# Chunked linear attention with a highway layer on one core: query rows of 2 KB, joint 64-row turns, compact state, gate in SBUF, a new order

## The chip, the core and the metric

The kernel runs on one core of a Trainium2 chip. Its engines have queues of their own and run beside each other: TensorE (PE; its weight loads are listed as PEld), VectorE (DVE), ScalarE (ACT), GpSimd (POOL) and SyncE (SP), which here issues DMAs. The metric is the device time of one execution in microseconds, as the median of several runs.

## What is computed

Four batches, eight heads, 768 positions, head size 64. Attention goes in blocks of 64 positions with a decay `lam` per head and a state that is carried from block to block; a highway layer follows on the 3072 x 512 result.

```python
for b in range(nb):                       # blocks of 64 positions
    qb, kb, vb = q[:, :, sl], k[:, :, sl], v[:, :, sl]
    intra = einsum('bhic,bhjc->bhij', qb, kb) * Dmask[None]      # lam**(i-j) for i >= j
    intra = einsum('bhij,bhjd->bhid', intra, vb)
    inter = einsum('bhid,bhde->bhie', qb * lam_pow[None], kv_state)
    out[:, :, sl] = intra + inter
    kv_state = lam_block * kv_state + einsum('bhsd,bhse->bhde', kb * rev_pow, vb)
# x: (B*S, H*D)
H = maximum(x @ w_h, 0);  T = sigmoid(x @ w_t + b_t)
result = T * H + (1 - T) * x
```

Inputs and the result are float32. The kernel may choose its own blocks: a mask with the decay and a carried state give the same result at any block length.

## The kernel before

The kernel splits each batch into three tiles of 256 positions, twelve tiles n in all, and each tile into two blocks b of 128. Within a tile, partition p holds positions 2p and 2p+1 (index j), so that one 512 B row of q, k or v (two positions of one head) goes to one partition, and block b is one half of the partitions. Instead of a decay matrix it scales queries by lam to the power t and values by lam to the power -t, t counted in the batch, in the cast from float32 to bf16 (`cast_q`, `cast_v`; `cast_k` only casts). The scores then need only a 0/1 mask `tri`, and the state is a plain sum that stays in one PSUM bank `kv` for a whole batch. Heads go in pairs hp, e being the head in the pair.

Steps of one tile:
- `load` of q, k and v, each in two halves of four heads (256 KB), all on SP's queue; `load_w` of the two weight matrices in halves of 512 KB.
- `trans` turns k and q with an identity on the full 128x128 array, eight per tile and operand; `evac_k` and `evac_q` copy them from PSUM, the second reordering positions.
- `score` and `state` run as 64x64 pieces of the array, interleaved in `scores_state`; `mask` multiplies scores by `tri` on DVE.
- `evac_s` copies the state (128x512, a head pair's own 64x64 blocks on the diagonal and zeros beside them), `inter` multiplies it with the queries, eight full-array matmuls per tile (none for the first block of a batch), and `intra` adds the masked scores times the values into the same bank `o`.
- `take` copies `o` to bf16 `xT`. The highway layer works on `xT` in four blocks per tile of eight matmuls each (`block`: h and t for each half u), then `relu` (DVE: max(h,0) - x), `sigm` (ACT, in place in PSUM), `gate` (DVE: times the sigmoid), and `turns` adds x and the gated part while turning back to rows; `evac_r` and `store_r` put out 512 KB per tile. The last tile goes in two halves, with `turn`, `evac_o` and `store`.

The order of every engine's work is written out by hand in the string PLAN. A token names a step, its arguments, the engine after @ and the PSUM banks after =: Lk, Lq, Lv loads; W, WC weights and their casts; CK, CQ, CV casts; TK, TQ turns; EK, EQ their evacuation; SS, S, U scores and state; KE state copy; M mask; I inter; A intra; D take; F block; H relu; G sigmoid; X gate; R turn back; E evacuation; ST store; Z filler matmuls on an all-zero tile. Each engine takes its instructions in the order of the string and waits, in order, for what each needs. Work tiles come from pools whose buffer counts are in BUFS, seven PSUM banks are numbered 0 to 6, and the eighth is `kv`.

Of the kernel before, what the change touches and what calls it, by code (L numbers as in the profile page):

```python
# [22 lines left out]
WC.0.1.0@POOL D.0.1@ACT Lv.2.1 WC.0.1.1@DVE Z.4=0 SS.1.0=01 M.1.1.1 I.1=35 KE.1.1@ACT Lv.2.0 F.0.0.0=4 WC.1.1.0@DVE PT
M.1.0.1 Lk.3.1 F.0.1.0=6 M.1.0.0 WC.1.0.0@POOL WC.1.0.1@ACT Lk.3.0 WC.1.1.1@DVE A.1.1 A.1.0 BC F.0.0.1=1 H.0.1 Lq.3.1
D.1.1@ACT H.0.0 D.1.0@ACT F.0.1.1=0 Lq.3.0 CQ.2.2@POOL F.1.0.0=2 Lv.3.0 G.0.1@ACT CK.2.2@DVE F.1.0.1=6 Lv.3.1
G.0.0@ACT X.0.1@DVE TQ.2.2=5 Lq.4.0 X.0.0@DVE TK.2.2=4 EQ.2.2@ACT CV.2.2@POOL F.1.1.0=3 Lq.4.1 EK.2.2@DVE G.1.0@ACT
H.1.0 SS.2.0=01 Lk.4.1 H.1.1 CK.3.2@POOL SS.2.1=54 Lk.4.0 M.2.0.1 F.1.1.1=2 KE.2.0@ACT M.2.1.0 Lv.4.0 TK.3.2=3 M.2.1.1
CQ.3.2@POOL G.1.1@ACT I.2=15 M.2.0.0 Lv.4.1 A.2.1 X.1.0@DVE A.2.0 Lk.5.0 R.0=40 D.2.0@ACT D.2.1@DVE CV.3.2@POOL
TQ.3.2=6 E.0.0@ACT Lk.5.1 F.2.1.1=1 E.0.1@ACT EQ.3.2@DVE Lq.5.1 EK.3.2@ACT X.1.1@DVE F.2.1.0=5 CQ.4.2@POOL Lq.5.0
R.1=40 H.2.1 SS.3.1=62 Lv.5.0 F.2.0.0=3 CK.4.2@POOL KE.3.0@ACT M.3.1.1 Lv.5.1 E.1.1@ACT M.3.1.0 SS.3.0=52 E.1.0@ACT  # L30
H.2.0 Lq.6.0 TQ.4.2=0 KE.3.1@ACT CV.4.2@POOL M.3.0.1 TK.4.2=6 G.2.1@ACT Lq.6.1 F.2.0.1=4 M.3.0.0 EQ.4.2@ACT EK.4.2@DVE
Lv.6.0 I.3=32 A.3.0 CK.5.2@POOL A.3.1 Lk.6.1 SS.4.1=56 D.3.0@ACT D.3.1@DVE TK.5.2=0 KE.4.0@ACT M.4.1.1 Lk.6.0
F.3.0.0=2 G.2.0@ACT CQ.5.2@POOL EK.5.2@DVE Lv.6.1 SS.4.0=36 H.3.0 F.3.0.1=0 Lq.8.0 M.4.0.0 CV.5.2@POOL M.4.0.1
TQ.5.2=2 Lk.9.0 G.3.0@ACT F.3.1.0=3 X.2.1@DVE Lq.7.0 EQ.5.2@ACT X.2.0@DVE F.3.1.1=6 CQ.6.2@POOL M.4.1.0 Lq.7.1
KE.4.1@ACT I.4=14 H.3.1 G.3.1@ACT R.2=25 Lk.8.1 X.3.0@DVE A.4.0 E.2.1@ACT X.3.1@DVE A.4.1 Lk.7.1 SS.5.0=30 E.2.0@ACT
D.4.0@DVE CK.6.2@POOL SS.5.1=56 D.4.1@ACT Lk.7.0 TQ.6.2=2 M.5.0.0 KE.5.0@ACT CV.6.2@POOL TK.6.2=1 M.5.1.1 Lv.7.0
EQ.6.2@ACT F.4.1.0=4 M.5.0.1 Lv.7.1 EK.6.2@ACT F.4.0.0=3 H.4.1 Lk.8.0 M.5.1.0 I.5=62 SS.6.1=01 H.4.0 Lq.8.1 A.5.0
KE.6.0@ACT M.6.1.0 CQ.7.2@POOL R.3=45 Lv.9.1 A.5.1 M.6.1.1 SS.6.0=30 D.5.0@ACT Lv.8.0 F.4.0.1=1 M.6.0.0 D.5.1@ACT
M.6.0.1 Lk.9.1 TQ.7.2=6 G.4.0@ACT CK.7.2@POOL F.5.0.0=3 Lq.10.1 EQ.7.2@ACT F.4.1.1=2 H.5.0 Lk.10.1 E.3.1@ACT X.4.0@DVE
TK.7.2=0 CV.7.2@POOL G.4.1@ACT I.6=63 ST.0 KE.6.1@DVE F.5.0.1=5 X.4.1@DVE Lv.8.1 F.5.1.0=1 G.5.0@ACT CK.8.2@POOL  # L40
EK.7.2@DVE Lq.9.0 A.6.0 E.3.0@ACT H.5.1 A.6.1 SS.7.1=20 Lq.9.1 D.6.0@ACT D.6.1@DVE TK.8.2=4 M.7.1.1 F.6.1.0=1 Lv.9.0
EK.8.2@ACT X.5.0@DVE CK.9.2@POOL F.6.1.1=6 KE.7.0@DVE Lk.10.0 CQ.8.2@POOL H.6.1 R.4=30 SS.7.0=54 Lk.11.1 E.4.0@ACT
F.5.1.1=1 E.4.1@ACT M.7.0.1 G.6.1@ACT ST.4 M.7.1.0 TK.9.2=3 Lq.10.0 M.7.0.0 TQ.8.2=0 G.5.1@ACT CV.8.2@POOL F.6.0.0=4
EQ.8.2@DVE Lk.11.0 KE.7.1@ACT X.5.1@DVE I.7=25 EK.9.2@ACT Lq.11.0 A.7.0 H.6.0 A.7.1 CQ.9.2@POOL SS.8.0=01 X.6.1@DVE
D.7.1@ACT Lv.10.1 SS.8.1=34 M.8.0.1 D.7.0@ACT F.6.0.1=6 KE.8.0@DVE Lq.11.1 CK.10.2@POOL F.7.0.0=5 M.8.1.0 G.6.0@ACT
M.8.1.1 ST.3 TQ.9.2=1 CV.9.2@POOL H.7.0 F.7.1.0=2 EQ.9.2@ACT Lv.10.0 X.6.0@DVE TK.10.2=3 M.8.0.0 ST.1 I.8=45
EK.10.2@ACT CQ.10.2@POOL H.7.1 SS.9.1=61 A.8.1 KE.9.0@ACT M.9.1.0 A.8.0 R.5=02 M.9.1.1 SS.9.0=36 CK.11.2@POOL
E.5.1@DVE F.7.0.1=1 KE.9.1@ACT M.9.0.1 E.5.0@ACT F.7.1.1=2 D.8.0@DVE D.8.1@ACT ST.5 CQ.11.2@POOL M.9.0.0 G.7.0@ACT
Lv.11.1 TK.11.2=6 Lv.11.0 I.9=04 F.8.1.0=5 EK.11.2@ACT ST.2 X.7.0@DVE TQ.10.2=3 G.7.1@ACT H.8.1 CV.10.2@POOL F.8.0.0=1
EQ.10.2@ACT R.6=65 H.8.0 A.9.1 X.7.1@DVE A.9.0 SS.10.1=31 D.9.0@ACT D.9.1@DVE F.8.1.1=2 E.6.1@ACT M.10.1.1 F.9.1.0=0  # L50
E.6.0@DVE G.8.1@ACT M.10.1.0 ST.6 TQ.11.2=4 CV.11.2@POOL KE.10.0@DVE F.9.1.1=5 EQ.11.2@ACT X.8.1@DVE SS.10.0=16
G.9.1@ACT H.9.1 R.7=32 M.10.0.1 KE.10.1@ACT F.8.0.1=4 X.9.1@DVE E.7.0@ACT M.10.0.0 E.7.1@ACT I.10=06 SS.11.0=53
# [365 lines left out]
```

## Time and profile before

| | |
|---|---|
| median of three runs | 110.14 us (109.15 to 110.21) |
| profiled execution | 107.8 us span |
| instructions | 4970 |
| read from HBM / written | 20.98 MB / 6.29 MB |
| score masks on DVE, 48 | 31.0 us, 680 ns each |
| scales of q and v on POOL, 23 | 42.6 us, some 1.9 us per 1024 columns |
| sigmoids on ACT, 52 | 22.0 us |
| matmuls of the highway layer, 416 | 49.5 us |
| filler matmuls, 45 | 12.4 us |

The span is the time from the first to the last instruction of one profiled execution. Busy time of an engine is the union of its instructions; matmuls overlap each other, so the length of one record is not its share of PE's time: the distance between starts is. A line such as L299 is a line of the kernel. An arrow `out<-in` names the tiles. A group's idle time is the time that its engine stood still just before its instructions.

### The profile page before, as it was taken

How to read it: one execution, taken by the hardware profiler on the slowest of the kernel's cores; microseconds unless marked ns; L12 is line 12 of the kernel's file. 1: busy time of each engine (PE TensorE's matmuls, PEld its weight loads, DVE VectorE, ACT ScalarE, POOL GpSimd, SP SyncE). 2: the span in 40 equal slices, each digit the busy share in tenths (PEclk: the TensorE clock that was granted, in tenths of full speed). 3: DMA queues.
4: the chain of work that ended last, by engine and by line, in shares of the span. 5: the costliest groups of instructions: out<-in, count | busy, mean ns of one | idle time of the engine just before them, and what ended most of it. 6: DMA issues, size and time to landing. Idle time of an engine off the chain costs nothing.

```text
span 107.8 us, 4970 instructions
## 1 busy us (share of the span) xinstructions
PE 99.5 (92%) x2190; PEld 80.7 (75%) x2190; DVE 83.5 (77%) x140; ACT 70.1 (65%) x129; POOL 55.6 (52%) x46
## 2 busy tenths in 40 slices
PE   4986999999999999999999999999999999999950
PEld 1332665588987888889879888979898788899940
DVE  1133495879798987999975997999977998958860
ACT  3303254685875588499568766957697798587940
POOL 6028340427977988689529583999593600000000
PEclk9999999999999999999999999999999999999998
DMA  0899999999999999999999999999999444108264
GB/s 3 221 302 289 291 357 384 327 286 284 290 298 264 298 280 303 284 293 263 288 277 272 297 333 285 294 272 303 361 325 290 152 182 161 40 6 317 78 240 149
DMA packets 42701, 27.59 MB, mean 256 GB/s; under 512 B 1588, under 2 KB 38712, under 8 KB 42680
## 3 DMA queue, kind: packets, MB, share of 16 engines
q1 hardware_dynamic: 42528, 27.27, 86.7%
q8 instruction: 17, 0.28, 1.0%
q14 instruction: 4, 0.03, 0.1%
q10 hardware_dynamic: 152, 0.01, 0.1%
HBM read 20.98 MB, written 6.29 MB: 253 GB/s over the span
## 4 chain that ended last, share of the span: by engine, by line
PE 74%; DVE 10%; DMA 5%; issue 3%; POOL 1%; SPq 1%; ACT 1%; POOLq 0%; DVEq 0%
PE bt L299 18%; PE bh L299 17%; PE bs L216 7%; PE bx L346 6%; PE bo L281 6%; DMA qf<-in_q_dram 5%; DVE m L255 5%; PE bqtr L203 5%; PE bspin L365 5%; PE bktr L203 4%; PE bo L271 3%; DVE hm L304 2%; DVE th L317 2%; PE kv L221 2%; POOL qb L189 1%
## 5 line engine op out<-in xcount | busy, mean ns | idle before, releaser
L299 PEld LDWEIGHTS <-w_b 128*128 128x128 bf16 x416 | 36.4, 98 | 5.0 <-issue 0.5
L255 DVE TENSOR_TENSOR m<-bs,tri 128x512 bf16<-128x512 f32 x48 | 31.0, 680 | 2.9 <-PE bs L216 2.3
L189 POOL TENSOR_TENSOR qb<-qf,pow_q 128x1024 bf16<-128x1024 f32 (+1 forms) x13 | 23.6, 1812 | 9.5 <-DMA qf<-in_q_dram 8.7
L313 ACT ACTIVATE bt<-bt,bt_col 128x256 f32<-128x256 f32 (+1 forms) x52 | 22.0, 432 | 7.5 <-PE bt L299 4.1
L299 PE MATMUL bh<-xT,w_b 128*128 128x256 bf16 (+1 forms) x208 | 25.0, 265 | 0.0
L299 PE MATMUL bt<-xT,w_b 128*128 128x256 bf16 (+1 forms) x208 | 24.5, 265 | 0.4 <-DVE th L317 0.2
L189 POOL TENSOR_TENSOR vs<-vf,pow_v 128x1024 bf16<-128x1024 f32 x10 | 19.0, 1902 | 7.4 <-DMA vf<-in_v_dram 6.5
L304 DVE SCALAR_TENSOR_TENSOR hm<-bh,xT 128x512 bf16<-128x512 f32 (+1 forms) x26 | 16.5, 643 | 3.3 <-PE bh L299 2.4
L317 DVE TENSOR_TENSOR th<-bt,hm 128x512 bf16<-128x512 f32 (+1 forms) x26 | 16.4, 642 | 2.0 <-ACT bt L313 1.9
L216 PE MATMUL bs<-qT,kT 64*64 64x128 bf16 x384 | 14.0, 218 | 0.4
L365 PE MATMUL bspin<-blank,id 128*128 128x512 bf16 x45 | 12.4, 420 | 1.4 <-POOL id masks.py:199 1.4
L103 POOL CAST kb<-kf 128x1024 bf16<-128x1024 f32 (+1 forms) x10 | 9.9, 994 | 7.1 <-DMA kf<-in_k_dram 7.1
L101 ACT ACTIVATE ss<-kv 128x512 bf16<-128x512 f32 x15 | 9.0, 597 | 6.3 <-PE bs L216 5.1
L216 PEld LDWEIGHTS <-kT 64*64 64x64 bf16 x384 | 10.9, 106 | 2.6 <-issue 1.1
L101 ACT ACTIVATE xT<-bo 128x512 bf16<-128x512 f32 x16 | 9.2, 597 | 4.8 <-PE bo L281 4.8
L101 ACT ACTIVATE o<-bx 128x512 f32<-128x512 f32 x19 | 10.5, 596 | 1.3 <-PE bx L346 1.3
L101 ACT ACTIVATE qT<-bqtr 128x1024 bf16<-128x1024 bf16 (+1 forms) x10 | 9.8, 980 | 1.8 <-PE bqtr L203 1.8
L281 PE MATMUL bo<-m,vs 64*64 64x128 bf16 x384 | 9.3, 219 | 0.7 <-DVE m L255 0.4
L365 PEld LDWEIGHTS <-id 128*128 128x128 bf16 x45 | 4.4, 106 | 6.6 <-issue 1.9
L221 PE MATMUL kv<-vs,kb 64*64 64x64 bf16 x320 | 9.3, 196 | 0.0
L203 PE MATMUL bqtr<-id,qb 128*128 128x128 bf16 x96 | 7.5, 220 | 0.9 <-POOL qb L189 0.9
L281 PEld LDWEIGHTS <-vs 64*64 64x64 bf16 x384 | 6.5, 106 | 2.4 <-issue 1.6
(50 smaller groups left out, 110.1 us busy)
## 6 DMA issues: line engine op xcount, KB each, us to landing
kf<-in_k_dram SPq DMA_DIRECT2D x24, 256.0 KB, 5.5
vf<-in_v_dram SPq DMA_DIRECT2D x24, 256.0 KB, 5.4
qf<-in_q_dram SPq DMA_DIRECT2D x24, 256.0 KB, 5.5
out_dram<-o SPq DMA_DIRECT2D x11, 512.0 KB, 3.8
w_f<-in_moe_w_h_dram SPq DMA_DIRECT2D x2, 512.0 KB, 6.6
w_f<-in_moe_w_t_dram SPq DMA_DIRECT2D x2, 512.0 KB, 8.6
out_dram<-oh SPq DMA_DIRECT2D x2, 128.0 KB, 2.0
out_dram<-oq SPq DMA_DIRECT2D x1, 256.0 KB
```

Source lines behind the costliest of these rows:

```text
L101: A.activation(dst, src, AF.Copy)
L189: ENG[eng].tensor_tensor(dst, in0=get(src, n)[:, heads(p)].rearrange("p h (j d) -> p h j d", j=J), in1=pw[:, n % NST, heads(p), :, None].t ...
L203: T.transpose(t[:, i, j, :], get(x + "b", n)[:, j, h:h + 2, :], id128)
L216: T.matmul(get("s", n, e, hp // 2)[half(b), hp % 2, j, :], lhsT=get("kT", n)[half(e), hp, j, half(b)], rhs=get("qT", n)[half(e), hp, b * C ...
L221: T.matmul(kv[half(e), hp, half(e)], lhsT=get("kb", n)[half(b), j, 2 * hp + e, :], rhs=get("vs", n)[half(b), 2 * hp + e, j, :], start=firs ...
L255: V.tensor_tensor(new(("m", n, e, u), [128, 2, J, C]), in0=get("s", n, e, u), in1=tri[:, None].to_broadcast([128, 2, J, C]), op=ALU.mult)
L281: T.matmul(get("o", n, b)[half(e), hp, :], lhsT=get("vs", n)[half(b), 2 * hp + e, j, :], rhs=get("m", n, e, u)[half(b), hp % 2, j, :], sta ...
L299: T.matmul(t[:, r, :], lhsT=w_b[w][:, kc, (2 * u + r) * 128:(2 * u + r + 1) * 128], rhs=get("xT", *g)[:, kc, :], start=(kc == 0), stop=(kc ...
L304: V.scalar_tensor_tensor(new(("hm", g, u), [128, 2, z * C], tag=f"hm{z}"), in0=get("h", g, u), scalar=0.0, in1=get("xT", *g)[:, 2 * u:2 * ...
L313: A.activation(dst[:, r, :], src[:, r, :], AF.Sigmoid, bias=bt_col[:, 2 * u + r:2 * u + r + 1])
L317: ENG[eng].tensor_tensor(new(("th", g), [128, NP, z * C], tag=f"th{z}")[:, 2 * u:2 * u + 2, :], in0=get("tt", g, u), in1=get("hm", g, u), ...
L365: T.matmul(t, lhsT=id128, rhs=blank, start=True, stop=True)
```

## The change

- Queries: partition p now holds eight positions of both heads of a pair, so that the row of a head is 2 KB. One load of 512 KB brings a whole tile (`load_q`). In a half of the partitions, p is made of 16 groups of eight positions and four head pairs.
- Turns: `trans_k` and `trans_q` work on halves of 64 partitions, 16 instructions each per tile, and write into two banks that k and q share, one per block b; `evac_kq` copies each bank (128x1024) in one go. Query positions lie in the order (t, group) afterwards; `tri` is built in that order and `take` puts it right.
- State: `kv` is 128x256, without the zero blocks; `inter` goes as 64x64 pieces, 16 per tile.
- Gate: the sigmoid writes a bf16 tile in SBUF, and 17 of 26 gates are on POOL, nine on DVE.
- lam comes as one row; a matmul with ones spreads it over the partitions (`spread`), and `powers` makes the two tables of powers, the query one per partition by a selection.
- Tiles that rotate are allocated once and taken in turn (`new`).
- PLAN is another order, with other engines for some steps and 25 fillers instead of 45; BUFS has other counts.

Counts by engine in the orders: EK and EQ 17 ACT and 9 DVE (four of the first tile's in halves) become EB 14 ACT and 10 DVE; D 16 ACT and 8 DVE become 21 and 3; E 20 ACT and 5 DVE become 14 and 11; whole-tile or half-tile CK 2 ACT, 1 DVE, 10 POOL become 6 ACT and 8 POOL.

```diff
 PLAN = """
-Lk.0.0 Lv.0.1 Lv.0.0 Lq.0.0 Lk.0.1 Lq.0.1 Lv.1.1 CK.0.0@POOL Lq.1.0 Z.12=0 TK.0.0=0 Lq.1.1 CV.0.0@DVE Lk.1.0
-CQ.0.0@POOL EK.0.0@DVE Lv.1.0 CV.0.1@DVE CK.0.1@ACT Lk.1.1 Z.11=1 TQ.0.0=1 B=2 EQ.0.0@ACT CQ.0.1@POOL W.0.1 W.0.0
...
-F.12.1.1=5 G.10.0@ACT X.10.1@DVE F.11.1.1=1 F.11.1.0=0 G.12.1@ACT X.10.0@DVE F.11.0.1=2 G.11.1@ACT H.11.1 F.12.1.0=4
-R.10=36 G.11.0@ACT H.12.1 X.11.1@DVE F.11.0.0=0 E.10.0@ACT X.12.1@DVE F.12.0.1=4 E.10.1@ACT H.11.0 F.12.0.0=1
-G.12.0@ACT X.11.0@DVE ST.10 R.11.1.1=5 H.12.0 R.11.0.2=3 E.11.1.1@DVE X.12.0@DVE E.11.0.2@ACT ST.11.1.1 R.11.1.0=0
-ST.11.0.2 E.11.1.0@DVE ST.11.1.0
+LM=0 PW Lv.0.0 Lv.1.0 Lk.0.0 Lq.0 CV.0.0@POOL CQ.0.1@DVE Lk.0.1 CQ.0.0@POOL CK.0.0@ACT Z.18=1 TQ.0=12 Lv.0.1 PT
+CV.0.1@DVE CK.0.1@POOL Lq.1 Lk.1.0 Lk.1.1 TK.0=12 EB.0.0@DVE Lv.1.1 EB.0.1@ACT Z.4=3 SS.0.1=34 W.0.1 CQ.1.1@DVE
+KE.0.0@ACT CQ.1.0@DVE CK.1.1@ACT M.0.1.1 Z.1=5 SS.0.0=56 CV.1.0@POOL M.0.1.0 M.0.0.1 I.0=01 TQ.1=24 CK.1.0@POOL TK.1=24
+B=3 CV.1.1@POOL KE.0.1@ACT WC.0.1.0@POOL EB.1.1@DVE EB.1.0@ACT Z.2=6 SS.1.1=64 M.0.0.0 W.0.0 Lq.2 A.0.0 Lk.2.0 A.0.1
+WC.0.1.1@POOL KE.1.0@DVE M.1.1.0 Lk.2.1 I.1=25 Lv.2.0 WC.0.0.0@POOL M.1.1.1 D.0.1@ACT WC.0.0.1@POOL D.0.0@ACT Lv.2.1
+SS.1.0=61 M.1.0.1 W.1.0 KE.1.1@ACT CQ.2.2@POOL F.0.0.0=0 M.1.0.0 H.0.0 W.1.1 A.1.1 WC.1.0.1@POOL F.0.1.0=4 Lq.3
...
+F.11.1.1=0 E.7.1@DVE ST.5 E.9.1@ACT E.8.1@ACT G.10.0 F.12.0.1=2 X.10.0@POOL F.12.0.0=1 F.11.1.0=3 G.11.1 E.8.0@DVE
+X.10.1@DVE H.12.0 F.11.0.0=5 ST.7 F.11.0.1=4 R.10=01 E.9.0@DVE H.11.0 F.12.1.0=6 H.11.1 G.12.0 X.11.1@POOL ST.8
+F.12.1.1=2 G.11.0 X.11.0@POOL X.12.0@DVE E.10.0@ACT E.10.1@DVE R.11.1.0=5 G.12.1 ST.9 E.11.1.0@ACT ST.10 ST.11.1.0
+H.12.1 R.11.0.2=3 E.11.0.2@ACT ST.11.0.2 X.12.1@DVE R.11.1.1=4 E.11.1.1@DVE ST.11.1.1
 """
-BUFS = dict(kf=5, qf=5, vf=5, kb=3, qb=2, vs=3, kT=2, qT=2, m=8, xT4=2, th4=2, xT2=3, xT1=2, th2=2, th1=2, hm2=3, hm1=2, tb2=2, tb1=2, ss=4, o=5, oh=2, oq=1)
+BUFS = dict(kf=5, qf=5, vf=5, kb=3, qb=3, vs=4, kq=3, m=8, xT2=4, xT1=2, th2=3, th1=2, hm2=4, hm1=4, tb2=4, tb1=4, ss=6, o=5, oh=2, oq=1)
...
-    kv = ps.tile([128, NP, 128], F32, tag="kv", name="kv", bufs=1)
-    V.memset(kv, 0.0)
+    kv = ps.tile([128, NP, D], F32, tag="kv", name="kv", bufs=1)
...
-            made[key] = sb.tile(shape, dtype, tag=tag, name=tag, bufs=BUFS[tag])
+            i = turn_of.get(tag, 0)
+            turn_of[tag] = (i + 1) % BUFS[tag]
+            if (tag, i) not in kept:
+                kept[tag, i] = singles.tile(shape, dtype, name=f"{tag}{i}")
+            made[key] = kept[tag, i]
...
+    def load_q(n):
+        b, c = divmod(n, NST)
+        nc.sync.dma_start(out=new(("qf", n), [128, 2, QT * D], F32),
+                          in_=q[b, :, c * 2 * C:(c + 1) * 2 * C, :].rearrange("h (g t) d -> g h (t d)", t=QT))
...
+    def trans_k(n, bk):
+        turn_banks(n, bk)
+        for hp in range(NP):
+            for j in range(J):
+                for b in range(2):
+                    i = (hp * J + j) * 64
+                    T.transpose(get("tr", n, b)[:, i:i + 64], get("kb", n)[half(b), j, 2 * hp:2 * hp + 2, :], id128[half(b), half(b)])
+
+    def trans_q(n, bk):
+        turn_banks(n, bk)
+        for t in range(QT):
+            for b in range(2):
+                T.transpose(get("tr", n, b)[:, KN:].rearrange("p (hp t g) -> p hp t g", hp=NP, t=QT)[:, :, t, :],
+                            get("qb", n)[half(b), t], id128[half(b), half(b)].rearrange("p (g hp) -> p hp g", hp=NP))
+
+    def evac_kq(n, b, eng):
+        copy(eng, new(("kq", n), [128, 2, 1024])[:, b], get("tr", n, b))
...
-        for b in range(2):
-            if n % NST or b:
-                for hp in range(NP):
-                    T.matmul(get("o", n, b)[:, hp, :], lhsT=get("ss", n, b)[:, hp, :],
-                             rhs=get("qT", n)[:, hp, b * C:(b + 1) * C],
-                             start=hp == 0, stop=False, skip_group_check=True)
-                begun.update((n, b, e) for e in range(2))
+        for hp in range(NP):
+            for x in range(2):
+                for e in range(2):
+                    b = e ^ x
+                    if n % NST or b:
+                        T.matmul(get("o", n, b)[half(e), hp, :], lhsT=get("ss", n, b)[half(e), hp, :], rhs=qT(n, b, hp)[half(e)],
+                                 start=o_first(n, b, e), stop=False, skip_group_check=True)
...
-        copy(eng, new(("xT", *g), [128, NP, z * C], tag=f"xT{z}")[:, :, r * C:(r + 1) * C], get("o", n, b))
+        copy(eng, new(("xT", *g), [128, NP, z * C], tag=f"xT{z}")[:, :, r * C:(r + 1) * C].rearrange("p h (g t) -> p h g t", t=QT),
+             get("o", n, b).rearrange("p h (t g) -> p h g t", t=QT))
...
+            A.activation(new(("tb", g, u), [128, 2, z * C], BF16, tag=f"tb{z}")[:, r, :], get("t", g, u)[:, r, :], AF.Sigmoid,
+                         bias=bt_col[:, 2 * u + r:2 * u + r + 1])
...
+    def spread(bk):
+        T.matmul(bank(("lm",), bk[0], [128, H]), lhsT=ones, rhs=lam_r, start=True, stop=True)
+
+    def powers():
+        A.activation(ln_bc, get("lm"), AF.Ln)
+        V.tensor_tensor(p_lnv, in0=ln_bc[:, None, :, None].to_broadcast([128, NST, H, J]),
+                        in1=tk_f[:, :, None, :].to_broadcast([128, NST, H, J]), op=ALU.mult)
+        A.activation(pow_v, p_lnv, AF.Exp, scale=-1.0)
+        V.tensor_tensor(ln_sel, in0=ln_bc.rearrange("p (hp e) -> p e hp", e=2), in1=sel[:, None, :].to_broadcast([128, 2, NP]), op=ALU.mult)
+        V.tensor_reduce(ln_q, ln_sel, axis=mybir.AxisListType.X, op=ALU.add)
+        V.tensor_tensor(p_lnq, in0=ln_q[:, None, :, None].to_broadcast([128, NST, 2, QT]),
+                        in1=tq_f[:, :, None, :].to_broadcast([128, NST, 2, QT]), op=ALU.mult)
+        A.activation(pow_q, p_lnq, AF.Exp)
```

More of the change, by code (lines that the diff above doesn't have):

```diff
@@ L23 @@
[L23 to L52, printed above, removed]
@@ new lines @@
+D.5.0@ACT M.6.1.1 CQ.8.2@POOL R.2=61 Lk.9.1 TQ.7=40 Lv.9.0 Lq.11 TK.7=40 CK.8.2@POOL CV.7.2@POOL EB.7.1@DVE R.3=53
+F.5.0.0=2 KE.6.0@DVE Lk.11.0 EB.7.0@ACT Lk.10.0 E.3.0@ACT E.2.0@ACT F.4.1.1=0 H.5.0 E.2.1@ACT G.4.1 X.4.1@POOL
+CV.8.2@POOL I.6=45 Lq.10 Lk.11.1 SS.6.0=62 M.6.0.1 F.5.1.0=1 KE.6.1@ACT E.3.1@ACT M.6.0.0 F.5.1.1=0 H.5.1 X.4.0@DVE
+Lv.10.1 G.5.1 SS.7.1=23 M.7.1.0 X.5.1@POOL A.6.1 A.6.0 TK.8=61 CQ.9.2@POOL D.6.0@DVE M.7.1.1 TQ.8=61 CK.9.2@POOL
+KE.7.0@ACT I.7=02 D.6.1@ACT SS.7.0=45 F.6.1.0=3 KE.7.1@DVE ST.1 CV.9.2@POOL EB.8.0@DVE H.6.1 M.7.0.0 EB.8.1@ACT
@@ L195, in cast_v @@
-    def cast_v(n, p, eng):
-        scale(n, p, eng, "vf", new(("vs", n), [128, H, J, D])[:, heads(p)], pow_v)
-    def trans(x, n, p, bk):
-        hs = heads(p)
-        t = bank((x + "tr", n, p), bk[0], [128, (hs.stop - hs.start) // 2, J, C], BF16)
-        for i, h in enumerate(range(hs.start, hs.stop, 2)):
-            for j in range(J):
-                T.transpose(t[:, i, j, :], get(x + "b", n)[:, j, h:h + 2, :], id128)
-    def evac_k(n, p, eng):
-        hs = heads(p)
-        copy(eng, new(("kT", n), [128, NP, J, C])[:, hs.start // 2:hs.stop // 2], get("ktr", n, p))
@@ L215, in score, with qT @@
+    def qT(n, b, hp):
+        i = KN + hp * C
+        return get("kq", n)[:, b, i:i + C]
     def score(n, e, hp, j, b):
-        T.matmul(get("s", n, e, hp // 2)[half(b), hp % 2, j, :], lhsT=get("kT", n)[half(e), hp, j, half(b)],
-                 rhs=get("qT", n)[half(e), hp, b * C:(b + 1) * C], start=True, stop=True)
+        T.matmul(get("s", n, e, hp // 2)[half(b), hp % 2, j, :], lhsT=kT(n, b, hp, j)[half(e)], rhs=qT(n, b, hp)[half(e)], start=True, stop=True)
     def state(n, b, hp, j, e):
@@ L234, in scores_state @@
                 state(n, b, *st[i])
-    def scores(n, u, bk):
-        for e in range(2):
-            bank(("s", n, e, u), bk[e], [128, 2, J, C])
-        for hp in (2 * u, 2 * u + 1):
-            for j in range(J):
-                for e in range(2):
-                    for b in range(2):
-                        score(n, e, hp, j, b)
     def states(n, b):
```

143 lines of the change are left out of this document (92 added, 51 removed).

## The prediction

> **What bounds the kernel now.** I read the page's busy shares and slices first, then five-microsecond windows and the waits, then the chain in order of time, then the timeline of TensorE alone.
>
> The page, its busy line and slices:
> ```profile
> PE 99.5 (92%) x2190; PEld 80.7 (75%) x2190; DVE 83.5 (77%) x140; ACT 70.1 (65%) x129; POOL 55.6 (52%) x46
> ...
> PE   4986999999999999999999999999999999999950
> ...
> DMA  0899999999999999999999999999999444108264
> GB/s 3 221 302 289 291 357 384 327 286 284 290 298 264 298 280 303 284 293 263 288 277 272 297 333 285 294 272 303 361 325 290 152 182 161 40 6 317 78 240 149
> ```
> The windows (length, then PE, PEld, DVE, ACT, POOL busy, clock, DMA share, GB/s):
> ```profile
> 5.00:10.00 5.00, 3.55 (x21) 1.42 (x19) 2.17 (x5) 1.00 (x3) 2.21 (x3) 1.00 1.17 302
> 15.00:20.00 5.00, 4.79 (x90) 2.75 (x82) 3.50 (x6) 2.60 (x3) 0.76 (x2) 1.00 1.06 381
> 25.00:30.00 5.00, 5.00 (x56) 4.39 (x55) 4.23 (x6) 3.76 (x8) 4.34 (x3) 1.00 1.07 290
> 55.00:60.00 5.00, 5.00 (x110) 4.55 (x103) 3.16 (x6) 3.98 (x8) 3.20 (x3) 1.00 0.98 284
> ```
> PE is full from about 20 to 101 us; idle in those windows adds up to 0.9 us. DMA is as full until 81 us, but PE doesn't wait for it there: the casts on POOL do. The list of waits (total, times, longest) has 22 us of that:
> ```profile
> POOL qb L189 <- DMA qf<-in_q_dram: 8.7, 6, 2.1
> POOL kb L103 <- DMA kf<-in_k_dram: 7.1, 4, 2.9
> POOL vs L189 <- DMA vf<-in_v_dram: 6.5, 6, 2.8
> ```
> So the middle is worth its PE work, and DMA and casts set only when it can begin. Before 21 us PE runs fillers (bspin, 45 recorded, 12.4 us).
>
> The chain in order of time (start, length, what) gives the price of each kind of PE work:
> ```profile
> 46.10 0.87 PE bh L299 x8
> ...
> 47.85 0.45 PE bo L271 x8
> 48.30 0.57 PE bx L346 x32
> 48.87 0.57 PE bo L281 x32
> ...
> 50.20 0.55 PE bqtr L203 x8
> 50.76 0.45 PE bktr L203 x8
> ```
> A full-array turn is 56 ns (0.45/8). The 0.55 beside 0.45 is a change of array shape, 0.10. The turns back (L346) start as pairs on two row halves; the timeline of PE shows them 29 ns apart, 0.47 for 32, the rest of 0.57 being such a change:
> ```profile
> 48.23 0.20 PE L346 MATMUL bx<-id,xT 64*128 64x64 bf16 x2
> 48.27 0.19 PE L346 MATMUL bx<-id,th 64*128 64x64 bf16 x2
> 48.30 0.19 PE L346 MATMUL bx<-id,xT 64*128 64x64 bf16 x2
> 48.33 0.19 PE L346 MATMUL bx<-id,th 64*128 64x64 bf16 x2
> ```
>
> **Part by part.** Sums are made against this execution (span 107.8); the median of 110.14 lies 2.3 above it, and I carry that over.
>
> *Joint turns.* Before, q and k take 8 turns each per tile: 24 groups x 0.45 = 10.8. After, each takes 16 of 64 rows, in pairs on two row halves with 64 moving columns, the shape of L346: 24 x 8 pairs x 29 ns = 5.6. **-5.2 us**, all on PE. For keys the row fits exactly. The query turns read the identity in steps of four and write PSUM in runs of 16; no PE row does that. Lower end: 29 ns a pair. Upper end: halves that don't overlap, each at the old 56 ns, 112 a pair, +83 ns x 96 pairs = +8.0. I take 29, the row of the same shape, and keep the upper end as a rival.
>
> *Inter as 64x64 tiles.* 80 full matmuls x 56 = 4.5 us become 160 small ones, which go two at a time (row and column half are the same). Nearest row: L281, 128 columns, four tiles at a time, 0.47/8 = 59 ns per group. So 80 x 59 = 4.7, **+0.2**; ends 2.4 (all four tiles) and 9.0 (no overlap).
>
> *Changes of array shape.* Counting neighbours in the written orders: 62 before, 70 after, **+0.8** at 0.10.
>
> *Evacuations.* Compact state: 20 copies fall from 512 to 256 columns; DVE 0.68 to 0.42 (the 128x256 copy of bx), ACT 0.60 to 0.38 (slope of L313: (450-339)/128 ns a column), 4.6 us of DVE and ACT time. Turns: still two 1024-column copies per tile, now contiguous: DVE 0.684, where the reordered query copy took 1.225; ACT 1.03 either way. The xT copies now read PSUM with a stride; f32 there already runs at 0.683, and ACT's reordered query copy (1.022) was no dearer than its plain one (1.032): 0, at most 0.54 x 3 on DVE. Sigmoids write bf16 to SBUF: 0.38 to 0.45. Summed by rows, DVE falls from 83.5 to some 79, ACT rises to some 72 (four more key casts at 1.06). PE's needs hide these; without that cover they would cost what each engine exceeds PE by.
>
> *Gates.* 26 on DVE at 0.64 become 9 on DVE (between 0.42, the 512-column SBUF cast, and 0.683) and 17 on POOL. POOL's two-input 512-column rows are 1.04 and 1.59; I take 1.04, the undisturbed one. POOL rises to about 66 of 103 us. POOL is in order: a gate can stand behind a 1.90 cast that waits for a load, and the turn back on PE, with all behind it, then waits too. In return the PSUM bank of bt is free after the sigmoid. I charge **+1.0**, as much again as the 0.9 of middle idle now; ends 0 and 6. The Trainium skill, GPSIMD Engine Reference, Engine selection, advises against elementwise work on POOL, about twice as slow with two inputs; the trace agrees in kind, 1.90 against DVE's 1.21 for the 1024-column scale, and by that rule alone the gates would be dearer, as already charged.
>
> *Loads.* 12 query loads of 512 KB in 2 KB rows replace 24 of 256 KB in 512 B rows. Casts that start on landing (5.53, 7.32, 8.27, 9.04) give 0.9 us per 256 KB. The slices at 357 and 384 GB/s are the weights, which already come in 2 KB rows: 512 KB in 1.42 against 1.81. Saves 12 x 0.39 = 4.7 us of DMA, no PE time: it keeps loads ahead of a faster PE. With no gain from the rows, loads would arrive about on time at tile 7, costing up to 1. Lasting tiles add no instruction; SP's waits for buffers were 4 us of an 80 us stream, so 0, ends -1 and +1.
>
> *Start.* Lam as a row puts a matmul at the head of PE that waits for that load (Ln began at 4.61), and behind it are the fillers, then the first turns. The fillers now start near 4.8, and the first ones come 0.43 apart (the trace's first ten), later 0.22: 18 of them end at 10.5. Powers: Ln, two Exps and four small DVE steps at 0.2, ready near 6.2 against 5.5; a dozen more set-up steps on DVE end before lam lands, and the kv memset (0.48) is gone. SP's order gives landings at 5.5, 6.4, 7.3 (k), 8.7 (q), 9.6, 10.5, 12.0 (q1), 12.9, 13.8, 14.7, then two weight halves 16.1 and 17.5, tile 2 until 22.5, the other weights 24.0 and 25.4. Query casts end near 9.8, under the fillers; turns 10.5 to 11.0, evacuation behind the value scale on DVE (10.5 to 11.2) until 11.9; first scores 12.0 (12.4 before). First dense block near 19 (22.3 before). POOL's cast of the late weights waits until 24.0 with tile 3's casts behind it, due near 31. The first T block can start at 26.1. Until then PE does six turn groups 1.4, six score-state groups 2.8 (0.47 each), inter 1.1, intra 0.9, four h blocks 3.5, 15 shape changes 1.5: 11.2 useful of 26.1, 14.9 lost. Before, 21.1 us held 4.4 useful, 16.7 lost. **-1.8**, ends -4 and +3.
>
> *Tail.* Before, 3.5 us from the last matmul to the end, after a short store; the same now. Stores are bunched: the last 2.6 MB at 370 GB/s takes 7 us, about what the last PE work leaves. 0, up to +1.
>
> Sum: -5.2 + 0.2 + 0.8 + 1.0 - 1.8 = -5.0; span 102.8, **about 105.1 us**.
>
> **Rivals.**
> 1. *Strided query turns* (slower). If a pair costs 112 ns, +8.0: 113.1. Slower than before from +52 ns a pair (5.0/96). For it: no row shows such a pattern. Against: runs of 16 are still contiguous. A milder form at 58 ns gives +2.8: 107.9. The Trainium skill, PSUM — Partial Sum Buffer, Specifications, says that any non-contiguous pattern slows matmuls significantly; no run here shows it yet.
> 2. *Gates behind casts.* If each of 11 turns back waits 0.5 us more for POOL, 5.5 of it returns: 109.6 with the 1.0 already charged, no change. For: POOL's 22 us of waits for loads. Against: it has a third of its time free, and turns back come late.
> 3. *A cold array.* Only 25 fillers remain. If the array falls to the first fillers' pace after gaps of 1 to 1.5 us near 14 to 18, four us of work cost two more: 107.1. Against: gaps of 0.5 and 0.9 us at 5.7 and 9.0 left the later fillers at 0.22.
>
> **How the numbers follow.** Forecast 0.65; strided, strong 0.10, mild 0.08; gates 0.10; cold 0.07. The forecast's own range is 102.3 to 107.5, from the start's ends and stalls. For 8 in 10 I add the mild forms and half of the gates: 102.3 to 109.3; outside remain strong strides 0.10, half the gates 0.05 and 0.05 below. One per cent is what a measurement here can tell: faster is below 109.0. Forecast, mild and cold with little left out, 0.78; within, most of the gates, 0.08; slower, strong strides and the gates' upper part, 0.14.
>
> **What would show it.** Right: query and key turns at 0.24 per 16, inter near 0.47, first dense block near 19, PE full from 26 until 97, query loads at 350 GB/s or more. Wrong: query turns above 80 ns a pair, PE waiting on POOL's th, or blocks of 1.7 us in place of 0.87.

## The result and the profile after

| | before | after |
|---|---|---|
| median of four runs each | 110.16 us | 118.02 us (117.04 to 120.47) |
| ratio | | 1.073 (1.067 to 1.078) |
| profiled execution, span | 107.8 us | 118.4 us |
| TensorE instructions (matmuls and weight loads) | 4380 | 4888 |

The changed kernel is slower by 7.3%; the prediction said 105.1 us. The profiled execution is the longest of its four (the others span 114.9 to 116.6 us), so some 2 to 3.5 us of the 10.6 between the two spans are its own; where it matters, other runs stand beside it.

The page of the changed kernel, its busy line, slices, queue of instruction fetches and chain:

```profile
PE 98.3 (83%) x2444; PEld 78.3 (66%) x2444; DVE 81.1 (68%) x138; ACT 66.0 (56%) x128; POOL 69.5 (59%) x64
...
PE   2994986979885898698999939999999999999920
...
PEclk9999999999999999999999996899999999999996
DMA  2999999999999999999999994001800005307690
...
q8 instruction: 19, 0.31, 1.0%
...
PE 61%; issue 11%; DVE 9%; DMA 5%; ACT 5%; POOL 3%; SPq 1%; POOLq 1%; DVEq 0%; ACTq 0%
```

PE has about as much busy time as before (98.3 against 99.5 us), and DVE, ACT and POOL are near the predicted sums. What is new is holes in PE's slices, and they are only where the DMA slices are full: when the loads end, at some 72 us, PE is full to the end. In the chain 11% of the span is "issue", time in which an engine waited for nothing that the profile knows; before it was 3%.

The same in windows (length, then PE, PEld, DVE, ACT, POOL busy, clock, DMA share, GB/s):

```profile
25.00:30.00 5.00, 4.81 (x94) 3.93 (x93) 4.87 (x8) 3.06 (x6) 1.68 (x2) 1.00 1.01 279
...
35.00:40.00 5.00, 2.95 (x65) 2.14 (x68) 3.02 (x6) 2.83 (x6) 4.00 (x4) 1.00 1.04 302
...
70.00:75.00 5.00, 3.77 (x69) 3.12 (x69) 1.81 (x4) 1.02 (x1) 5.00 (x5) 0.67 0.50 174
75.00:80.00 5.00, 5.00 (x149) 4.38 (x148) 3.89 (x7) 2.68 (x6) 2.59 (x2) 0.99 0.01 3
```

The chain in order of time, at the largest hole but one (start, length, what):

```profile
36.68 0.33 PE bt L334 x2
37.01 1.98 issue
38.99 0.81 PE bt L334 x6
...
42.18 0.57 PE btr L244 x16
42.75 0.24 PE btr L238 x16
```

PE stops for 1.98 us after two of the eight matmuls of one block: same bank, same input, nothing to wait for. PE's next holes in the chain end at 44.91, 50.56, 55.11, 65.31 and 71.23, after 0.72, 1.38, 0.36, 0.27 and 2.06 us. Two earlier ones, of 1.17 and 0.75 us, begin at 17.55 and 23.62. Not every "issue" of a chain is a hole of PE:

```profile
58.27 0.15 DVE th L350
58.42 1.71 issue
60.12 0.69 DVE hm L339
```

This one stands between two steps of DVE. A gate there runs from 58.19 for 2.02 us, and PE works meanwhile; it stops for 0.22 us at 60.64, waiting for the second of the two. Windows from 0 to each of five of PE's holes count the matmuls before it:

```profile
0.00:18.70 18.70, 13.17 (x222) 7.35 (x223) 10.68 (x30) 7.19 (x11) 12.15 (x23) 1.00 0.94 299
0.00:24.30 24.30, 17.93 (x350) 11.08 (x351) 14.14 (x36) 10.21 (x16) 14.21 (x26) 1.00 0.96 306
0.00:38.90 38.90, 29.42 (x606) 20.34 (x607) 27.73 (x52) 19.25 (x32) 24.24 (x32) 1.00 0.99 308
0.00:44.85 44.85, 34.62 (x734) 24.48 (x735) 32.02 (x59) 23.11 (x40) 27.63 (x34) 1.00 1.00 309
0.00:50.50 50.50, 38.89 (x862) 27.84 (x863) 34.95 (x63) 26.18 (x46) 30.70 (x36) 1.00 1.00 311
```

222, 350, 606, 734, 862: steps of exactly 128 matmuls (between the second and the third of them, two), and with a weight load each, 256 instructions. The other three end at 990, 1246 and 1374, and at 1118, in the same steps, two matmuls start 0.29 us apart. The queue of instruction fetches brings 19 packets of 16 KB for 4888 TensorE instructions, and 17 for the 4380 of before: a packet is 256 instructions. In the trace such a packet begins some 2.4 us ahead of the end of a hole (36.5 for 38.99, 42.5 for 44.91, 48.3 for 50.56). So the theory of the experiments: TensorE runs out of instructions. From 38.99 to 71.23 the holes end 32.24/6 = 5.4 us apart, and that is what 256 instructions take here while loads run. The kernel before used 1767 instructions between 35 and 70 us, 256 in 5.1 us, and has one such hole there, 0.23 us at 54.07, behind matmul 990; its other longer stretches of "issue" stand between steps of DVE. It is close to the edge.

One wait for another engine is there too, earlier. The chain at 29 us:

```profile
27.92 1.28 DVE m L289 x2
29.20 1.13 DVE qb L216
30.33 2.04 DVE th L350
32.37 0.60 DVE m L289
```

The last line is the next mask: it stands behind a gate of 2.04 us, which takes 0.41 at 43.66, where POOL is idle.

Where both kernels stand at 35 us decides how this is to be read. The groups of PE's instructions up to 35 us have the same work in both: 66 and 64 matmuls of the highway layer, 96 scores, 96 intra products, the turns of four tiles, 32 turns back. Everything that the change does ahead of 35 us, the two early holes included, comes out even, and the loss comes after it: from 35 us to the last matmul 69.3 us before, 78.3 after. From the last matmul to the end it is 3.5 and 5.1 us.

### The profile page after: what moved, and what is told of

It reads as the page before. It is cut to its first block, busy times and chain, and to the rows that moved or that the text cites. A ratio compares the mean times of both kernels' runs of the same rounds, so it can differ in the third digit from the quotient of the medians.

```text
span 118.4 us, 5498 instructions
## 1 busy us (share of the span) xinstructions
PE 98.3 (83%) x2444; PEld 78.3 (66%) x2444; DVE 81.1 (68%) x138; ACT 66.0 (56%) x128; POOL 69.5 (59%) x64
## 4 chain that ended last, share of the span: by engine, by line
PE 61%; issue 11%; DVE 9%; DMA 5%; ACT 5%; POOL 3%; SPq 1%; POOLq 1%; DVEq 0%; ACTq 0%
PE bh L334 17%; PE bt L334 13%; PE bs L260 9%; DMA qf<-in_q_dram 5%; PE bo L315 5%; PE btr L244 5%; PE bo L307 4%; PE bx L379 3%; DVE th L350 3%; PE btr L238 3%; DVE hm L339 2%; DVE m L289 2%; ACT kq L99 2%; PE kv L264 2%; POOL qb L216 1%
## 5 line engine op out<-in xcount | busy, mean ns | idle before, releaser
L350 POOL TENSOR_TENSOR th<-tb,hm 128x512 bf16<-128x512 bf16 (+1 forms) x17 | 18.9, 1118 | 29.0 <-ACT tb L345 13.7
L345 ACT ACTIVATE tb<-bt,bt_col 128x256 bf16<-128x256 f32 (+1 forms) x52 | 20.8, 460 | 15.4 <-PE bt L334 14.4
L223 POOL TENSOR_TENSOR vs<-vf,pow_v 128x1024 bf16<-128x1024 f32 (+1 forms) x11 | 19.3, 1758 | 2.1 <-DMA vf<-in_v_dram 1.4
L99 ACT ACTIVATE kq<-btr 128x1024 bf16<-128x1024 bf16 x14 | 14.0, 1023 | 10.5 <-PE btr L238 6.2
L216 POOL TENSOR_TENSOR qb<-qf,pow_q 128x1024 bf16<-128x1024 f32 (+1 forms) x9 | 17.1, 1902 | 3.8 <-DMA qf<-in_q_dram 3.7
L260 PE MATMUL bs<-kq 64*64 64x128 bf16 x384 | 17.4, 222 | 2.0 <-issue 1.7
L260 PEld LDWEIGHTS <-kq 64*64 64x64 bf16 x384 | 13.4, 108 | 3.0 <-issue 1.7
L244 PE MATMUL btr<-id,qb 64*128 64x64 bf16 x192 | 8.1, 232 | 3.8 <-issue 2.2
L101 POOL CAST kb<-kf 128x1024 bf16<-128x1024 f32 (+1 forms) x8 | 8.9, 1118 | 3.1 <-ACT ss L99 3.1
L264 PEld LDWEIGHTS <-kb 64*64 64x64 bf16 x320 | 8.9, 108 | 2.2 <-issue 2.2
L350 DVE TENSOR_TENSOR th<-tb,hm 128x512 bf16<-128x512 bf16 (+1 forms) x9 | 8.7, 968 | 1.1 <-ACT tb L345 1.1
```

Of the source, the lines that this page charges most:

```text
L99: A.activation(dst, src, AF.Copy)
L216: ENG[eng].tensor_tensor(new(("qb", n), [128, QT, 2, D])[:, ts].rearrange("p t e d -> p e t d"), in0=get("qf", n).rearrange("p e (t d) -> ...
L223: ENG[eng].tensor_tensor(new(("vs", n), [128, H, J, D])[:, hs], in0=get("vf", n)[:, hs].rearrange("p h (j d) -> p h j d", j=J), in1=pow_v[ ...
L244: T.transpose(get("tr", n, b)[:, KN:].rearrange("p (hp t g) -> p hp t g", hp=NP, t=QT)[:, :, t, :], get("qb", n)[half(b), t], id128[half(b ...
L260: T.matmul(get("s", n, e, hp // 2)[half(b), hp % 2, j, :], lhsT=kT(n, b, hp, j)[half(e)], rhs=qT(n, b, hp)[half(e)], start=True, stop=True)
L264: T.matmul(kv[half(e), hp, :], lhsT=get("kb", n)[half(b), j, 2 * hp + e, :], rhs=get("vs", n)[half(b), 2 * hp + e, j, :], start=first, sto ...
```

## The experiments

Times are medians, beside runs of the kernel before on the same chip: 109.39 us for the first four runs, 109.45 for the next four, 109.44 for the three after, 109.79 for the last.

**Fewer loads in flight.**
```diff
-BUFS = dict(kf=5, qf=5, vf=5,
+BUFS = dict(kf=3, qf=3, vf=3,
```


> The changed kernel with 3 instead of 5 buffers for the loaded q, k and v, so that loads are issued as casts free buffers and fewer transfers stand in DMA's queues. Theory F: PE stands still where its instruction stream crosses a block of 256 instructions (128 matmuls) while the next block's fetch waits in the DMA engines behind loads; the long gaps in the trace of the changed kernel (1.17, 0.75, 1.98, 0.72, 1.38, 2.06 us) are these. It expects the gaps at the block edges to sum to less than half of now (some 10 us) and a time of 114 or less. Rival D: PE waits for data, from DVE and POOL, which hinder each other. It expects no gain, 118 or more, since loads only come later.

118.79 us, ratio 1.085 (1.074 to 1.096). Holes of 0.75, 1.23, 0.84, 0.91, 1.10 and 1.51 us stay, again at steps of 128 matmuls, in a profiled execution of 114.8 us: they do not belong to a long execution alone. The DMA slices are full until 70 us as before but for one dip at 55 us, so the time tells nothing of the traffic; the holes tell a little. Of the seven steps that end between 35 and 70 us, the five with a hole had a DMA share of 0.91 to 1.14 in the 3 us before it. Of the two without, one comes right behind the dip, at 0.47, and the other, at 42.8, had 1.09. With two buffers instead of three:

> The changed kernel with 2 instead of 5 buffers for loaded q, k and v (3 did not change the load on DMA until 70 us). Theory F: if DMA's share falls below 0.9 in 25 to 75 us, the gaps shrink and the time is 112 to 116; where loads then come too late, POOL's and ACT's waits for DMA grow and take that back. Rival D: 119 or more.

122.1 us, ratio 1.096 (1.088 to 1.105). In the written order loads then come into tiles before their last reader, so this computes from other data; and loads are now late: the chain has a stretch from 56.6 to 63.6 in which SP's queue and a load of keys are waited for, 7 us that hide everything else. So the time is inconclusive too. Here the traffic is thinned in places, though, and the holes follow it. Nine steps of 128 matmuls end between 35 and 90 us. The four with a hole (2.15, 0.30, 0.58 and 1.24 us) had a DMA share of 0.92 to 1.08 in the 3 us before it. Of the five without, four had 0.19 to 0.61, and the fifth, at 65.4 with 1.01, comes behind a wait of PE of 4.78 us for the loads.

**Empty instructions in the kernel before.** The one kernel that has no part of the change:
```diff
             for kc in range(KC):
+                T.nop("pad")
```


> The kernel before, with one empty instruction in front of each of the 416 matmuls of the highway layer: 1.6 more blocks of 256 instructions on PE, no more work in the array. Theory F: a block takes some 5.3 us to arrive while loads run (blocks landed at 16, 21, 26, 36, 42, 48 us in the changed kernel), so 4 to 8 us are added and gaps appear at block edges. Rival D: at most 1 us.

116.21 us, ratio 1.063 (1.055 to 1.071): 6.8 us for 416 instructions that do nothing. Its chain has holes of PE as in the changed kernel, and the fetch queue again 19 packets:

```profile
q8 instruction: 19, 0.31, 1.3%
```
```profile
42.23 0.56 issue
...
57.33 0.96 issue
...
68.75 0.27 issue
...
87.98 0.22 PE bh L300 x2
88.20 1.56 issue
89.75 0.82 PE bh L300 x6
```

A fifth hole of PE, 1.26 us at 51.83, is not on the chain. Before the first hole come 684 matmuls, as many weight loads and 96 empty instructions, 1464 in all; before the others 1977, 2232, 2744 and 3767. That is 256, or twice or four times as many, from one to the next, give or take the one record that is missing. The empty instructions cost nothing where they stand: a block of eight matmuls takes 0.87 us with them as without. The last hole comes beside the last two loads and a store, at a DMA share of 0.86 in the 3 us before. So a larger number of TensorE instructions makes a loss of nearly this size by itself, without any of the new shapes, gates or orders.

**Query turns without steps.** Identity and PSUM contiguous; scores and inter read the queries in steps of four elements instead:
```diff
-                T.transpose(get("tr", n, b)[:, KN:].rearrange("p (hp t g) -> p hp t g", hp=NP, t=QT)[:, :, t, :],
-                            get("qb", n)[half(b), t], id128[half(b), half(b)].rearrange("p (g hp) -> p hp g", hp=NP))
+                i = KN + t * 64
+                T.transpose(get("tr", n, b)[:, i:i + 64], get("qb", n)[half(b), t], id128[half(b), half(b)])
...
-        i = KN + hp * C
-        return get("kq", n)[:, b, i:i + C]
+        return get("kq", n)[:, b, KN:].rearrange("p (t g hp) -> p hp t g", t=QT, hp=NP)[:, hp]
```


> The changed kernel with query turns that read the identity and write PSUM without steps; the steps go to the queries that scores and inter read (groups of 16 in steps of four). Theory S: the stepped turn is what makes 16 query turns take 0.48 us against 0.23 of the key turns; they fall to 0.23, 2.9 us less of PE work in all. If steps cost on the moving side, scores (0.47 for 16 beside 16 state pieces) and inter (0.57) grow instead. If only writes to PSUM cost, they stay, and the time falls by up to 3 where PE is the bound (after 75 us), by 1 in all; under theory F little of it is seen in the loaded part.

124.17 us, ratio 1.131 (1.121 to 1.142). The turns of queries fall from 0.48 per 16 to 0.23, as fast as those of keys, but the steps cost more where they went. Groups of this run (busy, mean ns of one, idle before):

```profile
L259 PE MATMUL bs<-kq 64*64 64x128 bf16 x384 | 28.8, 289 | 1.1 <-ACT kq L99 0.6 <-issue 0.2
...
L306 PE MATMUL bo<-kq,ss 64*64 64x128 bf16 x160 | 12.6, 289 | 0.0
```

Scores are at 17.4 us and inter at 7.9 in the changed kernel. Queries are the moving operand there, so reading it in steps of 8 bytes is what costs: 1.6 to 1.7 times in these sums, which run beside other work, twice in the turns. It is cheapest where fewest columns move, in the turns.

**All gates on DVE.** Seventeen tokens like X.3.1@POOL become X.3.1@DVE.

> The changed kernel with all 26 gates on DVE. Rival D, as contention for a port of SBUF: DVE's two-input steps beside POOL's take up to 2.07 us (0.41 alone) and POOL's 1.90 casts up to 2.73. With 17 gates less on POOL the steps slow each other less, and the turns back come earlier: 115 or less. Theory F: the gaps at block edges stay, 117 to 119.

120.01 us, ratio 1.085 (1.073 to 1.097); POOL falls from 69.5 to 50.7 us, DVE rises to 88.5. PE's holes at steps of 128 matmuls are still there, 1.30, 0.75, 1.74, 0.19, 0.36 and 0.68 us, so gates on POOL are not what makes them, and moving them gains nothing.

**The changed kernel without later loads.** The changed kernel itself, run again beside this and the next:

> The changed kernel once more, unchanged, beside the next ones. 117 to 119; again gaps of 0.7 us or more on PE at distances of 128 matmuls until the loads are through, and none after.

119.15 us (114.15 to 120.49). And with loads for tiles 0 to 4 only; tiles 5 to 11 work on the rows of those (`load_q` gets the same lines):
```diff
     def load(x, n, p):
+        if n >= 5:
+            made[x + "f", n] = get(x + "f", n - 5)
+            return
```


> The changed kernel with loads for the first five tiles only; tiles 5 to 11 compute from the buffers of the first five, so the output is that of other data. All work on the engines stays. DMA falls idle near 35 us. Theory F: with no loads in front of them, instruction blocks come in time; the gaps after 35 us vanish, PE is full from there, and the time falls to 106 to 111. Rival D (DVE and POOL hinder each other, or the order is bad): POOL and DVE do the same work, so the time falls by at most 2.

111.47 us (109.32 to 113.14), ratio 1.018 (1.013 to 1.024): 7.7 us less than the changed kernel beside it by the medians, 4.8 by the fastest runs, with the same instructions on every engine. The stretch from 35 to 70 us, the changed kernel first and then this run:

```profile
35.00:70.00 35.00, 29.10 (x810) 23.44 (x811) 26.61 (x40) 22.33 (x43) 23.53 (x17) 1.00 1.03 317
```
```profile
35.00:70.00 35.00, 34.28 (x1003) 28.88 (x998) 31.13 (x48) 24.89 (x48) 30.73 (x20) 1.00 0.14 49
```

810 matmuls become 1003 in the same time when DMA is at 49 GB/s and not at 317. The control is the same edit in the kernel before:

> The kernel before, with loads of q, k and v for tiles 0 to 4 only; tiles 5 to 11 are computed from the data of those tiles, so the output is of other data. The control to the same edit in the changed kernel, which took 7 us off. Theory (TensorE's instructions come late only where more than about 256 are wanted per 5.4 us while loads run): the kernel before is just at that rate, PE was busy 79.1 of 80 us between 20 and 100, so there is less than 1 us to gain in the middle: 107.5 to 109.5. Rival (the loads slow everything, through the memory that the engines share): the edit gains here what it gained in the changed kernel, 5 to 7 us: 102 to 104.

108.8 us, ratio 0.994 (0.991 to 0.997). The loads cost the kernel before 0.6 us and the changed one 7.7 (4.8 by the fastest runs): they do not slow the engines in general, they slow what the changed kernel wants more of.

**Fewer TensorE instructions, more array work.** Both kinds of turn on the full array, queries put in order in the evacuation, the 128x512 state with its zero blocks, inter on the full array; 544 TensorE instructions less (the expectations say 552):
```diff
-                for b in range(2):
-                    i = (hp * J + j) * 64
-                    T.transpose(get("tr", n, b)[:, i:i + 64], get("kb", n)[half(b), j, 2 * hp:2 * hp + 2, :], id128[half(b), half(b)])
+                i = (hp * J + j) * C
+                T.transpose(get("tr", n, 0)[:, i:i + C], get("kb", n)[:, j, 2 * hp:2 * hp + 2, :], id128)
...
+                    T.matmul(get("o", n, b)[:, hp, :], lhsT=get("ss", n, b)[:, hp, :], rhs=qT(n, b, hp),
+                             start=hp == 0, stop=False, skip_group_check=True)
```


> The changed kernel with turns and inter on the full array as in the kernel before: 8 instead of 16 turns each for k and q, 8 inter instead of 16 (state 128 wide again), queries reordered in their evacuation. 552 PE instructions less, 2.2 blocks. PE's work in the array by the measured rows: keys 0.45 against 0.23, queries 0.45 against 0.48, inter 0.45 against 0.57: +0.8 us in all; the reordering copy costs DVE up to 0.54 more each. Theory F: 4 to 8 us faster than the changed kernel, 110 to 114. By array work alone, or rival D: 118 to 120.

113.04 us (112.36 to 114.73), ratio 1.031 (1.025 to 1.036), 6.1 us less than the changed kernel beside it by the medians but only 1.8 by the fastest runs; the other seven of the changed kernel's eight took 117.0 or more. Then only the turns undone, inter left as 64x64 pieces:

> The changed kernel with the turns of keys and queries on the full array again, eight instructions of each per tile in place of 16; inter stays as 64x64 pieces. 384 TensorE instructions go (with their weight loads), and the turns take more of the array: 16 full turns took 0.91 us per tile in the version with turns and inter on the full array, the 32 half turns here 0.72, so 12 x 0.19 = 2.3 us more. Theory (instruction supply): of the 552 instructions that took 5.5 us off with turns and inter together 384 go here, so 3.8 us: 113.5 to 116.5. Rival (the array's time decides): 2.3 us more than the changed kernel, 119.5 to 122. A second rival (the 64x64 pieces of inter are what costs): no change, 117.5 to 119.5.

113.59 us, ratio 1.036 (1.027 to 1.046), at the lower edge of what the theory said and well below both rivals: 2.3 us more of array work, 384 instructions less, and 4.4 us gained on the changed kernel's first median. The two were not run side by side; by the ratios, 1.036 against 1.073 with intervals that do not meet, it is 4.0. The stretch from 35 to 70 us is full again, with the loads at 338 GB/s:

```profile
35.00:70.00 35.00, 34.11 (x830) 28.68 (x823) 32.40 (x46) 23.58 (x46) 29.09 (x20) 1.00 1.07 338
```

Behind 36 us PE has no hole left at a step of 128 matmuls; its one stop there, 0.75 us at 55.78, is a wait for DVE. The 160 further instructions that inter gave up in the run before gained nothing measurable. That fits the theory (once TensorE wants its blocks no faster than they come, fewer do not help) but does not show it: the version of the next run, with 160 instructions less, still has one such hole behind 36 us in each of two profiles, 0.48 and 0.80 us.

**The wait at 29 us.** In the version with both on the full array, the last mask of tile 2 put ahead of the scale and the gate:
```diff
-M.2.1.1 I.2=60 CK.3.2@POOL M.2.0.1 F.1.0.1=5 M.2.0.0 G.1.0 CV.3.2@POOL F.1.1.1=4 CQ.3.2@DVE X.1.0@DVE F.0.0.1=3 G.1.1
-G.0.0 M.2.1.0 F.0.1.1=1 A.2.0 A.2.1 Lk.4.1 CQ.4.2@POOL TQ.3=54 Lv.4.1 X.1.1@DVE D.2.1@DVE TK.3=54 Lk.5.0 D.2.0@ACT
+M.2.1.1 I.2=60 CK.3.2@POOL M.2.0.1 F.1.0.1=5 M.2.0.0 M.2.1.0 G.1.0 CV.3.2@POOL F.1.1.1=4 CQ.3.2@DVE X.1.0@DVE F.0.0.1=3 G.1.1
+G.0.0 F.0.1.1=1 A.2.0 A.2.1 Lk.4.1 CQ.4.2@POOL TQ.3=54 Lv.4.1 X.1.1@DVE D.2.1@DVE TK.3=54 Lk.5.0 D.2.0@ACT
```


> The version with turns and inter on the full array (113.04), and one mask of tile 2 (M.2.1.0) put ahead of the query scale of tile 3 and the first gate on DVE. In that version the mask waited from 29.0 to 33.6 us behind a scale of 2.58 and a gate of 2.04, PE stood still for 2.4 us, and then ran 35 to 40 us at a granted clock of 0.66. Theory (what is left of the loss is this one wait and the clock after it): 2.4 us and about 1.7 us of clock go, so 109 to 111. Rival (another input is late at the same place, or the instruction supply takes the time): under 1 us goes, 112 to 113.5.

113.71 us, ratio 1.037 (1.029 to 1.044): no gain, the rival was right. The chain shows what is late in the mask's place:

```profile
26.07 1.88 DVE m L290 x3
27.94 2.80 DVE qb L217
30.75 3.33 DVE th L350 x2
34.08 0.61 DVE xT L101
```

The whole of DVE from 26 to 34.7 us is one chain, and its two-input steps in SBUF take 2.80 for a scale and 3.33 for two gates, beside POOL's scales and gates; whichever order they have, PE's turn back or next block waits for the last. The next text expects what all gates on DVE would add:

> As the run before, and all 26 gates on DVE in place of nine. Theory (gates on POOL slow the two-input steps of DVE and put POOL's casts back): another 0 to 1.5 us goes, 108 to 110.5, and the POOL sum falls by some 18 us. Rival (gates on POOL cost nothing where they are, and DVE with 8 us more is what is late): 0 to 2 us slower than the run before.

112.78 us, ratio 1.035 (1.029 to 1.042). But the kernel that ran is that of the run before, character for character: its 17 gates are on POOL, and POOL is busy for 69.8 us, against 70.2. So this is the same kernel a second time, 0.9 us from the first, which shows how far two such medians can lie apart. It says nothing of the theory or of the rival; what gates on DVE do in this version is not known.

From 35 us to the last matmul, one profiled execution of each (all but one stand at the same work at 35 us, within four highway matmuls; the changed kernel without later loads is 1.4 us ahead, by eight such matmuls and 16 scores):

| | TensorE instructions | 35 us to last matmul | span of this execution | median of its runs |
|---|---|---|---|---|
| before | 4380 | 69.3 us | 107.8 us | 110.16 us |
| before, no later loads | 4380 | 68.5 us | 106.9 us | 108.8 us |
| before, empty instructions | 4796 | 75.7 us | 115.2 us | 116.21 us |
| after | 4888 | 78.3 us | 118.4 us | 118.02 us |
| after, three buffers | 4888 | 75.7 us | 114.8 us | 118.79 us |
| after, no later loads | 4888 | 67.4 us, 68.8 with the 1.4 | 107.4 us | 111.47 us |
| after, full turns | 4504 | 71.0 us | 109.7 us | 113.59 us |
| after, full array, mask early | 4344 | 70.7 us | 110.6 us | 113.71 us |

Against three buffers, which has the instructions of after, the stretch is 4.6 us shorter with full turns and 6.8 or more without later loads. No version that computes the result beats the kernel before.

## Why the prediction was wrong

**The step that failed** is the one that everything stands on: "the middle is worth its PE work, and DMA and casts set only when it can begin". PE in the middle is worth the larger of its array work and its instructions at the pace at which they come, and DMA has a hand in the second. The working priced 192 pairs of turns and 80 of inter at so many ns each, and never counted that they are 544 more instructions (508 with the fillers that go). The kernel before stood close to the limit: it has one short hole while loads run, without later loads it gains 0.6 us, and with 416 empty instructions it loses 6.8. PE's holes in the profiled execution from 37 to 71 us sum to 6.8 us, and the array comes back cold from the last of them: the granted clock is 0.50 from 71.7 to 75.1 us (0.67 in the window from 70 to 75), and a block there takes 1.70 us in place of 0.87. By an estimate from these, 3.4 us at half the clock cost up to 1.7 us. That makes up to 8.5 of the 9.0 us by which the stretch from 35 us to the last matmul is longer; before, such holes were 0.2 us of it.

**Joint turns, -5.2:** mis-sized. Keys take 0.24 per 16, as said; queries 0.48 (0.57 with the change of shape), 60 ns a pair instead of 29. So 12 x (0.45 + 0.45) becomes 12 x (0.24 + 0.48), -2.2 us. This is the mild form of the first rival, to which the text gave 0.08. The run with contiguous query turns shows that the steps make it. The recorded reason against this rival, that runs of 16 are still contiguous, did not help. The page of the Trainium skill that the prediction named for this, PSUM — Partial Sum Buffer, Specifications, says that a non-contiguous pattern slows matmuls; the runs agree in kind, with a factor of two, but the run with contiguous turns moved the steps to the moving operand in SBUF and kept the cost, so that they do not show PSUM as its place.

**Inter, +0.2:** 16 pieces take 0.56, 70 ns a pair, so +1.1. **Changes of shape, +0.8:** not measured apart. With these the array gains some 0.3 us in all, and not the 4.2 of the text; without later loads the two kernels' profiled spans are indeed alike, 107.4 and 106.9 us (the medians, 111.47 and 108.8, are not).

**Evacuations, 0:** right as a cost; the sums were near, DVE 81.1 (said: 79), ACT 66.0 (72), state copies on ACT 385 ns (0.38).

**Gates, +1.0:** the sum on POOL was right (69.5 against 66), the mechanism not. PE did not wait for a gate on POOL behind a cast. Of the gates left on DVE three took 1.5 to 2.1 us beside POOL's scales and gates, which made one wait at 29 us and 0.2 us at 60. The second rival did not happen: PE's list of waits has no gate on POOL.

**Start, -1.8:** first scores at 12.6 (said: 12.0), first dense block at 20.2 (19), behind the hole of 1.17 us at 17.55; that hole, the one of 0.75 at 23.62 and the wait at 29 us took the rest: at 35 us nothing is gained.

**Loads, 0:** the rate rose, to 317 GB/s from 290 between 35 and 70 us, less than the 350 that the text has for query loads, and loads end at 72 instead of 81 us. As a cost on PE this step was wrong: TensorE's instructions come late beside this traffic. **Tail, 0 up to +1:** 5.1 against 3.5 us in the two profiles, 3.7 to 5.1 in other runs of the new order.

**A cold array** came, but late and as a consequence, behind a hole of 2.06 us, and not at 14 to 18 us for want of fillers. Of the signs named for right, query turns at 0.24 and "PE full from 26 until 97" failed; of those for wrong only a block of 1.7 us came, behind the hole at 71 us. The range ended at 109.3, since no case in it had a limit on the number of instructions; the profile of before has the signs of one, 17 packets of a small queue and a hole of 0.23 us, and the working passed them over.

**What stays open.** The versions with full turns are still 3 to 4% slower than before. In the profile with full turns alone, 1.9 us longer than that of before, 1.8 us lie between 35 us and the last matmul; with the full array and the mask early 1.4 lie there and 1.4 in the tail. No run took these apart. The changed kernel's time lies between 114.15 and 120.49 us over eight runs, and no run shows why it varies so. Nor is it shown what in the load traffic holds the fetches up, its bytes, its packets or the order in a shared engine: the two runs with fewer buffers show only that the holes go with the DMA share. Nor is 5.4 us for 256 instructions a measured limit: it is what this kernel got, and the kernel before drew 256 per 5.1 us at 290 GB/s with one hole of 0.23.

## What to carry to other kernels

Before splitting TensorE work into smaller pieces, count instructions per microsecond in the stretch where loads run, each matmul with its weight load, and compare with what the kernel sustains there now: pieces of 30 ns can be free on the array and still be paid for in instructions. "Issue" gaps in the middle of a run of matmuls, 256 instructions or a multiple of it apart, are the sign (an "issue" in a chain can also stand between steps of another engine: look at what is on both sides of it); an empty instruction per matmul in the old kernel, and the new kernel without its loads, tell within two runs whether it is that. When a strided access is removed from one step, look at which step gets it.
